# Where in the queue early loads stand, and four DMA transposes in place of eight, in an attention + two-MoE kernel

## The chip, the core and the metric

The kernel runs on one core of a Trainium2 chip. The metric is device time in microseconds (us), the median of several runs. Engines: TensorE (PE), VectorE (DVE), ScalarE (ACT), GpSimd (POOL), and SyncE (SP), whose queue issues nearly all DMAs.

## The reference

```python
mask = q_bucket[:, :, :, None] == k_bucket[:, :, None, :]
scores = np.where(mask, scale * np.matmul(q, k.transpose(0, 1, 3, 2)), -1000000000.0)
attn = np.exp(scores - np.max(scores, axis=-1, keepdims=True))
attn = attn / (np.sum(attn, axis=-1, keepdims=True) + 1e-09)
x = np.matmul(attn, v)
...
h = x @ w_in
g = np.where(h > 0.0, h, alpha * (np.exp(np.minimum(h, 0.0)) - 1.0))
x = g @ w_out
...
h = x @ w_in2
r = np.maximum(h, 0.0)
out = (s * (r * r) + b) @ w_out2
```

Attention has 2 batches, 8 heads, 768 tokens, head size 64; a bucket is the 6 sign bits of a token's projection, and a token attends only to tokens of its own bucket. Both MoE stages have 1536 tokens, 512 columns and 2048 hidden columns. The weights of both stages are float64 in memory; the other inputs are float32.

## The kernel before

**Precision.** Products run in float16 with a high and a low part (hi, lo) of each operand, three matmuls for one product. Names ending in h and l are such parts.

**Attention.** The heads of a batch come in four pairs (hp 0 to 3). `p_load` (L252) loads q, k or v of a pair; `p_split` makes hi and lo (L260, L262, L265) and issues DMA transposes to k and q (L283, L284, L292); `p_bits` (L320, L323) and `p_buck` (L333, L337) make the mask as extra columns of k and q. A unit is one head of one chunk of 128 tokens, 96 in all. Its steps: scores s (L364), row maximum p (L375) and its scaling mx (L376), exp (L377), then the transposed weights pt, then `u_av`: xacc = pt x v. The first 16 units (chunks 0 and 1) transpose on PE (L386, L389, L414, reading v itself). The others split into ph hi (ACT L396) and lo (POOL L399), go through a DMA transpose pt<-ph (L401), and use 18 matmuls with vv, the split v (L420). After the last head of a chunk `u_norm` divides (L434 to L438), makes xh (hi L450, lo on POOL L451) and puts it by DMA transposes into a token buffer xx[i] (512 tokens each, three buffers x0, x1, x2): for chunks 0 and 1 by four transposes of 2 x 128 x 128 each time (L457), for the others by one (L459). Batch 1's first pairs are loaded into the last token buffer as a guest.

**Weights of the first MoE.** `w_stream` brings w_in and then w_out in chunks of 512 KB: `w_load` (L167) loads a chunk into one of WRAW = 3 buffers wraw, DVE joins the two words of each float64 to a float32 wa (L194, L195, L197), ACT makes hi (L188), and the low part is made on DVE (L204), or, for the first ASIDE = 12 chunks of a stream, scaled and subtracted on POOL (L187, L202). A load waits until DVE is done with its buffer.

**MoE.** `moe1` runs six blocks of 256 tokens: h (L551 with wi), the activation (L559 to L574), x2p (L551 with wo), written back to the token buffers. `up2` and `down2` are the second MoE.

**What sets the order.** The program is traced in the order of the generators: the main loop steps attention and pulls one weight chunk per step until chunks 0 and 1 are done, then interleaves MoE and attention by costs. A scheduler of the compiler then puts each engine's instructions into one fixed order. Each engine runs its list in order, and so does SP's queue: a DMA that must wait holds all behind it.

```python
for _ in att:
    n += 1
    if n >= W_FROM and n % WN == 0:
        next(ws1, None)
    if done_chunks[0] == BLOCKS1[0]:
        break
...
aside_ = n_ - 3 < aside
```

Of the kernel before, what the change touches and what calls it, by code (L numbers as in the profile page):

```python
# [8 lines left out]
F16 = mybir.dt.float16  # L9
BF16 = mybir.dt.bfloat16  # L10
I32 = mybir.dt.int32
# [52 lines left out]
W_FROM = 3  # L64
LN2 = 0.6931471805599453


def model_kernel(tc, q, k, v, proj, w_in, w_out, w_in2, w_out2, s2, b2, sel, pop, eye, out):
# [24 lines left out]
    with ExitStack() as base:  # L93
# [62 lines left out]
        def w_col_chunks(dst, dram):  # L156
            w = dram.bitcast(I32)
            return [([z[:, f:f + 4, 128 * d:128 * d + 128] for z in dst],
                     w[128 * f:128 * f + 512, 256 * d:256 * d + 256].rearrange("(k p) n -> p k n", p=128))
                    for d in range(KM) for f in range(0, KF, 4)]  # L160

        def w_load(ch, wraw):
            t = wraw.tile([128, 512, 2], I32, tag="w", name="wraw")
            o = t.rearrange("p n t -> p (n t)")
            if len(ch[1].shape) == 3:
                o = o.rearrange("p (k n) -> p k n", k=ch[1].shape[1])
            nc.sync.dma_start(out=o, in_=ch[1])  # L167
            return t

        def w_stream(chunks, wraw, words, delay=0, aside=0):  # L170
            loaded, joined = [], []
            for n_, ch in enumerate(chunks + [None] * 3):
                with late_by(delay):
                    done = joined.pop(0) if joined else None
                    if done:
                        (dst, _), w = done
                        w = w.bitcast(F32)
                        if callable(dst):
                            dst = dst(w)
                            done = dst and (None, w)  # L180
# [8 lines left out]
                    if len(loaded) == 2 or (ch is None and loaded):  # L189
# [4 lines left out]
                        nc.vector.tensor_scalar(x, top, 3, 0x3FFFFFFF, op0=ALU.logical_shift_left, op1=ALU.bitwise_and)  # L194
# [47 lines left out]
        def p_load(b, hp, nm):  # L242
# [9 lines left out]
            nc.sync.dma_start(out=t, in_=a[b, 2 * hp:2 * hp + 2].rearrange("h (p c) d -> p h (c d)", c=C))  # L252
# [56 lines left out]
        def p_bits(b, hp):  # L309
# [13 lines left out]
            nc.vector.tensor_scalar(t, p, 0.0, None, op0=ALU.is_gt)  # L323
# [106 lines left out]

        def u_norm(ch):
# [7 lines left out]
            if ch < FC:  # L439
                xh = per.tile([128, FC, 2, H * D // FC], F16, tag="xh", name="xh")  # L440
                fl = xf.rearrange("p (c h) d -> p c (h d)", c=FC)
                hi, lo = xh[:, :, 0, :], xh[:, :, 1, :]
            else:
                xh = per.tile([128, 2, H * D], F16, tag="xh", name="xh")
                fl = xf.rearrange("p h d -> p (h d)")
                hi, lo = xh[:, 0, :], xh[:, 1, :]
# [12 lines left out]
            nc.sync.dma_start_transpose(out=xx[ch // 4][:, :, ch % 4 * 128:ch % 4 * 128 + 128], in_=xh.rearrange("p x d -> p (x d)"))  # L459
# [130 lines left out]
        def moe1(wi, wo, gp, next_gp, tmp, tmpg, att_step):  # L590
# [13 lines left out]
            def up(i):  # L604
# [7 lines left out]
                for f0 in range(0, KF, w_):  # L612
                    p = ring.take("m", [128, 512], F32, "h")
                    for f in range(f0, f0 + w_):
                        xs = [lambda kk, o=o: xx[i2][:, o + kk, o2:o2 + n] for o in (0, KM)]
# [9 lines left out]
            def down(i):  # L625
# [4 lines left out]
                for d0 in range(0, KM, w_):  # L630
                    p = ring.take("m", [128, w_, n], F32, "x2p")
                    for d in range(d0, d0 + w_):
                        xs = [lambda kk, z=z: z[:, kk, :] for z in g[i]]
                        ws = [lambda kk, w=w: w[:, kk, d * 128:d * 128 + 128] for w in wo]
                        for part in range(4):
                            products(p[:, d - d0, :], ws, xs, range(4 * part, 4 * part + 4), KF)
                            if part == 3 and d == d0 + w_ - 1:
                                xh, xl = (xx[i2][:, z * KM + d0:z * KM + d0 + w_, o2:o2 + n] for z in range(2))
# [52 lines left out]
        def up2(wi, g, ps_y, stream, fed, fed_all, ahead):  # L691
# [12 lines left out]
            for f in range(KF):  # L704
# [3 lines left out]
                for i in range(len(g)):  # L708
                    p = ring.take("m", [128, 512], F32, "h")
                    xs = [lambda kk, o=o: xx[i][:, o + kk, :] for o in (0, KM)]  # L710
# [118 lines left out]
        if True:  # L829
# [12 lines left out]
            n = 0  # L842
# [21 lines left out]
            ws1 = chain(ws1, w_stream(w_col_chunks(wo, w_out), *wdec))  # L864
# [135 lines left out]
```

## Time and profile before

| | |
|---|---|
| median of 3 runs | 716.72 us (714.48 to 717.6) |
| the profiled execution | 715.42 us, its span 713.6 us |
| busy share of the span | PE 92%, PEld (weight load) 70%, DVE 73%, ACT 58%, POOL 37% |
| DMA | 89.72 MB, queue of SP 57.2% of 16 engines |

The profile is one execution. Its times count from the start of the span. A row of the timeline has start, duration, engine, line, operation and tiles, and in brackets the idle time before it and what ended that. A row of stretches gives busy us of each engine in it, the granted PE clock as a share of full speed, the busy share of the DMA engines and GB/s.

### The profile page before, as it was taken

To read this page: it belongs to the slowest core of one execution; us is meant where nothing else is said; L and a number is where in the kernel's file an instruction comes from. 1 tells how busy PE (TensorE), PEld (TensorE's weight loads), DVE (VectorE), ACT (ScalarE), POOL (GpSimd) and SP (SyncE) were. 2 spreads that over 40 slices of the span, in tenths; PEclk is the share of its full clock that TensorE was granted. 3 is DMA by queue.
4 is the path that set the end of the run, shared out by engine and by line. 5 is a ranking of instruction groups with operands and counts; after the bars stand their busy time and mean duration, and the time that the engine had idled before them with its cause. 6 is when DMAs were issued, how large, how long until landed. Compare 5 with 4: busy or idle time off the path is not lost.

```text
span 713.6 us, 15219 instructions
## 1 busy us (share of the span) xinstructions
PE 656.3 (92%) x6192; PEld 501.4 (70%) x6192; DVE 521.4 (73%) x893; ACT 417.0 (58%) x687; POOL 264.8 (37%) x211
## 2 busy tenths in 40 slices
PE   2588979979888999999999999999999999999998
PEld 0367757768666777888888988874444446888887
DVE  5899999989677467745744699439999626999730
ACT  2879769867687778656755333234545525555520
POOL 0247668764444378845854421311211200000000
PEclk9899989999999999999999999999999999999999
DMA  9994689999999499766768545003443000000100
GB/s 211 325 221 139 167 197 247 217 215 211 194 217 177 82 139 169 123 119 123 123 113 117 136 155 173 1 30 119 128 143 114 0 1 1 16 31 31 45 30 30
DMA packets 206933, 89.72 MB, mean 126 GB/s; under 512 B 172048, under 2 KB 203536, under 8 KB 206864
## 3 DMA queue, kind: packets, MB, share of 16 engines
q1 hardware_dynamic: 206272, 88.63, 57.2%
q8 instruction: 48, 0.79, 0.5%
q10 hardware_dynamic: 592, 0.14, 0.1%
q14 instruction: 21, 0.17, 0.1%
HBM read 43.13 MB, written 3.15 MB: 65 GB/s over the span
## 4 chain that ended last, share of the span: by engine, by line
PE 53%; ACT 4%; DVE 4%; DMA 2%; issue 2%; POOL 1%; DVEq 0%; ACTq 0%; POOLq 0%; SPq 0%
PE h L551 23%; PE y L795 15%; PE x2p L551 10%; PE s L364 3%; PE xacc L420 2%; DVE e L566 1%; DMA pt<-ph 1%; DVE g L568 1%; ACT ph L396 1%; ACT gh L571 1%; ACT p L377 1%; POOL ph L399 1%; ACT e L559 1%; DMA wraw<-in_moe_w_in 1%; DVE p L375 1%
## 5 line engine op out<-in xcount | busy, mean ns | idle before, releaser
L399 POOL TENSOR_TENSOR ph<-p,ph 128x768 f16<-128x768 f32 x80 | 133.4, 1671 | 84.3 <-ACT ph L396 54.8
L551 PE MATMUL h<-x,wih 128*128 128x256 f16 x768 | 130.4, 274 | 0.6 <-DVE g L568 0.6
L551 PE MATMUL h<-x,wi 128*128 128x512 f16 x576 | 124.5, 379 | 0.0
L377 ACT ACTIVATE p<-p,mx 128x768 f32<-128x768 f32 x96 | 89.2, 929 | 52.3 <-DVE mx L376 42.2
L375 DVE TENSOR_SCALAR_CACHE_REDUCE p<-s 128x768 f32<-128x768 f32 x96 | 91.1, 951 | 34.2 <-PE s L364 32.4
L795 PE MATMUL y<-wqh,a 128*128 128x256 f16 x672 | 110.3, 273 | 0.0
L795 PEld LDWEIGHTS <-a 128*128 128x128 f16 x1008 | 98.6, 98 | 11.7
L551 PE MATMUL x2p<-gh,woh 128*128 128x256 f16 x384 | 104.7, 273 | 1.4 <-ACT gh L571 0.8
L551 PE MATMUL x2p<-gl,woh 128*128 128x256 f16 x384 | 104.8, 273 | 1.1 <-POOL gl L574 1.0
L551 PE MATMUL h<-x,wil 128*128 128x256 f16 x384 | 105.2, 274 | 0.0
L551 PE MATMUL x2p<-gh,wol 128*128 128x256 f16 x384 | 104.6, 273 | 0.0
L551 PEld LDWEIGHTS <-wi 128*128 128x128 f16 x576 | 56.3, 98 | 67.8
L795 PE MATMUL y<-wql,a 128*128 128x256 f16 x336 | 91.1, 273 | 0.0
L364 PE MATMUL s<-k,q 128*128 128x512 f16 (+1 forms) x384 | 81.1, 336 | 6.9 <-DVE p L375 5.6
L551 PEld LDWEIGHTS <-wih 128*128 128x128 f16 x768 | 74.8, 98 | 13.0 <-issue 1.5
L551 PEld LDWEIGHTS <-woh 128*128 128x128 f16 x768 | 74.9, 98 | 12.7 <-issue 1.0
L574 POOL TENSOR_TENSOR gl<-g,gh 128x512 f16<-128x512 f32 x48 | 57.5, 1198 | 64.0 <-ACT gh L571 63.8
L420 PE MATMUL xacc<-vv,pt 128*128 128x64 f16 x1440 | 57.3, 194 | 20.0 <-DMA pt<-ph 19.9
L396 ACT ACTIVATE ph<-p 128x768 f16<-128x768 f32 x80 | 66.6, 836 | 13.7 <-DMA pt<-ph 10.0
L420 PEld LDWEIGHTS <-pt 128*128 128x128 f16 x1440 | 52.8, 99 | 28.6 <-DMA pt<-ph 26.0
L587 DVE SCALAR_TENSOR_TENSOR g<-h,sbs,r 128x512 f32<-128x512 f32 x48 | 35.6, 744 | 23.6 <-ACT r L584 23.6
L364 PEld LDWEIGHTS <-q 128*128 128x128 f16 x384 | 34.7, 101 | 25.6 <-issue 9.7
(118 smaller groups left out, 1027.7 us busy)
## 6 DMA issues: line engine op xcount, KB each, us to landing
wraw<-in_moe_w_in SPq DMA_DIRECT2D x32, 512.0 KB, 4.0
wraw<-in_moe_w_out SPq DMA_DIRECT2D x32, 512.0 KB, 3.8
out<-y SPq DMA_DIRECT2D x10, 256.0 KB, 2.0
raw<-in_k SPq DMA_DIRECT2D x6, 384.0 KB, 4.6
raw<-in_q SPq DMA_DIRECT2D x6, 384.0 KB, 5.8
v<-in_v SPq DMA_DIRECT2D x4, 384.0 KB, 8.8
pt<-ph SPq DMA_TRANSPOSE x80, 4.1
x<-in_k SPq DMA_DIRECT2D x2, 384.0 KB, 7.3
```

The lines of the kernel that those rows point to most:

```text
L364: nc.tensor.matmul(p[:, a0:a1], w[b, hp][:, j, c, :], kf[:, a0:a1], start=(x == 0), stop=(x == 1))
L375: nc.vector.tensor_scalar(f, sps.pop(u), CLAMP, None, op0=ALU.min, op1=ALU.min, accum_out=mx)
L377: nc.scalar.activation(out=f, in_=f, func=ACTF.Exp, scale=-sm / (SQ * SQ), bias=mx, accum_out=sums[gr][:, sl:sl + 1])
L396: nc.scalar.activation(out=t[:, 0, :], in_=f, func=ACTF.Copy)
L399: nc.gpsimd.tensor_tensor(out=t[:, 1, :], in0=f, in1=t[:, 0, :], op=ALU.subtract)
L420: nc.tensor.matmul(acc, o[:, C * x + cc, :], vv[:, j, cc, y, :], start=(z == 0 and cc == 0), stop=(z == 2 and cc == C - 1))
L551: nc.tensor.matmul(p, ws[a](kk), xs[b](kk), start=(kk == 0 and z == 0), stop=(kk == n_kk - 1 and z == 2))
L559: nc.scalar.activation(out=t["e"], in_=p, func=ACTF.Exp, scale=1.0 / SG)
L566: nc.vector.tensor_scalar(t["e"], t["e"], SG, -SG, op0=ALU.mult, op1=ALU.add)
L574: nc.gpsimd.tensor_tensor(out=gl, in0=t["g"], in1=gh, op=ALU.subtract)
L587: nc.vector.scalar_tensor_tensor(out=g, in0=p, scalar=sb["s"], in1=t["r"], op0=ALU.mult, op1=ALU.mult)
L795: nc.tensor.matmul(p, a[:, xa, kk, :], wq[y][:, WQ[n], kk, :], start=first and k == 0, stop=k == 3 * K2 - 1, skip_group_check=True)
```

## The change

It makes four edits.

1. Six loads are queued behind a given load of w_in (`HOLD`, by the number of the weight load): the four v of batch 0 behind loads 3, 3, 5 and 6, and the guests k and q of batch 1 behind loads 8 and 9. One DVE instruction of the first chunk (the first of the join) is queued behind the bits of head pair 1.
2. The first two chunks of w_out are loaded into the second token buffer, which nothing uses yet, behind weight loads 10 and 11 (`HOLD_E`, `w_early`), and handed to the w_out stream as already loaded. The stream's count `n_ - 3 < aside` is then true for these two, so that their scaling and low part run on POOL.
3. In a token buffer the hi and lo parts of x stand in another order (`xb`): blocks of 128 columns come as two hi, two lo, two hi, two lo.
4. With that, chunks 0 and 1 need two transposes of 4 x 128 x 128 each time in place of four of 2 x 128 x 128.

```diff
+HOLD = {(0, 0, "v"): 3, (0, 1, "v"): 3, (0, 2, "v"): 5, (0, 3, "v"): 6, (1, 0, "k"): 8, (1, 0, "q"): 9}
+HOLD_E = [10, 11]
...
+        w_loads, pins = [], {}
+        def behind(n):
+            return tc.issue_after(w_loads[n]) if n is not None else nullcontext()
...
-            nc.sync.dma_start(out=o, in_=ch[1])
+            w_loads.append(nc.sync.dma_start(out=o, in_=ch[1]).ins)
...
+        def w_early(ch, x):
+            t = xx[1].rearrange("p a t -> p (a t)").bitcast(I32)[:, 1024 * x:1024 * x + 1024]
+            with behind(HOLD_E[x]):
+                nc.sync.dma_start(out=t.rearrange("p (k n) -> p k n", k=ch[1].shape[1]), in_=ch[1])
+            return ch, t.rearrange("p (n t) -> p n t", t=2)
...
-        def w_stream(chunks, wraw, words, delay=0, aside=0):
-            loaded, joined = [], []
+        def w_stream(chunks, wraw, words, delay=0, aside=0, loaded_=None, late_dst=False):
+            loaded, joined = list(loaded_ or ()), []
...
-                        nc.vector.tensor_scalar(x, top, 3, 0x3FFFFFFF, op0=ALU.logical_shift_left, op1=ALU.bitwise_and)
+                        with tc.issue_after(pins["bits", 0, 1]) if n_ == 2 and loaded_ is None else nullcontext():
+                            nc.vector.tensor_scalar(x, top, 3, 0x3FFFFFFF, op0=ALU.logical_shift_left, op1=ALU.bitwise_and)
...
-            nc.sync.dma_start(out=t, in_=a[b, 2 * hp:2 * hp + 2].rearrange("h (p c) d -> p h (c d)", c=C))
+            with behind(HOLD.get((b, hp, nm))):
+                nc.sync.dma_start(out=t, in_=a[b, 2 * hp:2 * hp + 2].rearrange("h (p c) d -> p h (c d)", c=C))
...
+        def xb(z, kk):
+            return 4 * (kk // 2) + 2 * z + kk % 2
...
-                    o = xx[0][:, :, 128 * c:128 * c + 128].rearrange("p (z k) t -> p z k t", z=2)
-                    for z in range(2):
-                        nc.sync.dma_start_transpose(out=o[:, z, k2 * ch:k2 * ch + k2, :], in_=xh[:, c, z, :])
+                    nc.sync.dma_start_transpose(out=xx[0][:, 2 * k2 * ch:2 * k2 * ch + 2 * k2, 128 * c:128 * c + 128],
+                                                in_=xh[:, c].rearrange("p z n -> p (z n)"))
...
+                if len(early) < len(HOLD_E) and len(w_loads) > HOLD_E[len(early)]:
+                    early.append(w_early(co1[len(early)], len(early)))
...
-            ws1 = chain(ws1, w_stream(w_col_chunks(wo, w_out), *wdec))
+            ws1 = chain(ws1, w_stream(co1[len(early):], *wdec, loaded_=early, late_dst=True))
```

**The order on SP, after the q load of head pair 3.** Before (k12, k22 and q12 are k and q of pair 2, v0 the four v, x2 the guest):

```order
L252 DMA v0_339<-in_v 128x2x384
L252 DMA v0_400<-in_v 128x2x384
L252 DMA v0_580<-in_v 128x2x384
L252 DMA v0_651<-in_v 128x2x384
L167 DMA wraw_308<-in_moe_w_in 128x4x256
L252 DMA x2_115<-in_k 128x2x384
L283 DMA_TRANSPOSE k12_347<-src_341 128x12x128
L167 DMA wraw_332<-in_moe_w_in 128x4x256
L284 DMA_TRANSPOSE k22_348<-srcl_344 128x6x128
L292 DMA_TRANSPOSE q12_356<-src_351 128x12x128
```

In the change, at the same place:

```order
L303 DMA_TRANSPOSE k12_347<-src_341 128x12x128
L304 DMA_TRANSPOSE k22_348<-srcl_344 128x6x128
L175 DMA wraw_308<-in_moe_w_in 128x4x256
L272 DMA v0_339<-in_v 128x2x384
L312 DMA_TRANSPOSE q12_356<-src_351 128x12x128
L272 DMA v0_400<-in_v 128x2x384
L303 DMA_TRANSPOSE k13_408<-src_402 128x12x128
L175 DMA wraw_332<-in_moe_w_in 128x4x256
L304 DMA_TRANSPOSE k23_409<-srcl_405 128x6x128
```

The transposes of pair 2 come first; the first v stands behind the fourth weight load (wraw_308), and the other two v and the guest come later in the list.

**The order on DVE at the first weight chunk** (wraw_226 is that chunk, bits_259 the bits of pair 1). Before:

```order
L295 COPY q21_199<-q11_197 64x768 x2
L194 TENSOR_SCALAR wx_284<-wraw_226 128x512
L195 SCALAR_TENSOR_TENSOR wx_284<-wraw_226,wx_284 128x512
L197 SCALAR_TENSOR_TENSOR wa_283<-wraw_226,wx_284 128x512
L323 TENSOR_SCALAR bits_259<-pbit_238 128x768
```

In the change:

```order
L315 COPY q21_199<-q11_197 64x768 x2
L343 TENSOR_SCALAR bits_259<-pbit_238 128x768
L213 TENSOR_SCALAR wx_284<-wraw_226 128x512
L297 COPY src_341<-src_341 128x12x64
L285 SCALAR_TENSOR_TENSOR srcl_344<-raw_272,src_341 128x6x64 x2
L395 TENSOR_SCALAR p_291,mx_292<-s_278 128x768
L285 SCALAR_TENSOR_TENSOR src_351<-raw_274,src_351 128x6x64 x2
L214 SCALAR_TENSOR_TENSOR wx_284<-wraw_226,wx_284 128x512
L396 TENSOR_SCALAR mx_292<-mx_292 128x1
L395 TENSOR_SCALAR p_334,mx_335<-s_319 128x768
L216 SCALAR_TENSOR_TENSOR wa_283<-wraw_226,wx_284 128x512
```

The bits stand ahead of the chunk, and the chunk's three passes are spread out between the splits of pair 2 and the first maxima.

**The order on POOL, at the sixth to eighth ph.** Before:

```order
L399 TENSOR_TENSOR ph_1189<-p_1184,ph_1189 128x768
L376 TENSOR_SCALAR mx_1233<-mx_1233 128x1
L376 TENSOR_SCALAR mx_1288<-mx_1288 128x1
L376 TENSOR_SCALAR mx_1347<-mx_1347 128x1
L399 TENSOR_TENSOR ph_1237<-p_1232,ph_1237 128x768
L574 TENSOR_TENSOR gl_1074<-g_1265,gh_1073 128x512
L399 TENSOR_TENSOR ph_1292<-p_1287,ph_1292 128x768
```

In the change:

```order
L419 TENSOR_TENSOR ph_1200<-p_1195,ph_1200 128x768
L396 TENSOR_SCALAR mx_1302<-mx_1302 128x1
L205 TENSOR_SCALAR wa_1132<-wa_1132 128x512
L419 TENSOR_TENSOR ph_1248<-p_1243,ph_1248 128x768
L205 TENSOR_SCALAR wa_1187<-wa_1187 128x512
L419 TENSOR_TENSOR ph_1306<-p_1301,ph_1306 128x768
L221 TENSOR_TENSOR wol_1070<-wa_1132,woh_1069 128x4x128
L396 TENSOR_SCALAR mx_1361<-mx_1361 128x1
L597 TENSOR_TENSOR gl_1072<-g_1276,gh_1071 128x512
L396 TENSOR_SCALAR mx_1394<-mx_1394 128x1
L221 TENSOR_TENSOR wol_1070<-wa_1187,woh_1069 128x4x128
```

Two scalings and two low parts of w_out (wa_1132, wa_1187) now stand among the ph.

## Rows read from the trace of the kernel before

**Rows 1.** Stretches: busy us of each engine (x instructions), PEclk, DMA share, GB/s.

```profile
20.00:84.00 64.00, 51.77 (x402) 39.58 (x397) 59.88 (x122) 51.66 (x86) 33.76 (x26) 0.95 0.80 217
50.00:80.00 30.00, 26.60 (x221) 21.53 (x220) 26.94 (x58) 25.27 (x43) 22.28 (x17) 1.00 0.52 152
84.00:96.00 12.00, 6.76 (x70) 4.82 (x69) 11.93 (x22) 7.01 (x12) 7.94 (x8) 0.88 0.86 167
96.00:160.00 64.00, 55.88 (x661) 44.57 (x660) 60.20 (x100) 52.69 (x95) 46.71 (x45) 0.95 1.07 223
110.00:120.00 10.00, 8.61 (x111) 6.83 (x109) 9.50 (x15) 8.99 (x17) 9.67 (x9) 1.00 1.23 264
160.00:240.00 80.00, 70.49 (x812) 56.16 (x811) 59.63 (x103) 61.50 (x102) 39.12 (x31) 0.99 0.98 186
301.00:713.60 412.60, 407.84 (x3498) 306.54 (x3497) 280.56 (x433) 190.85 (x307) 93.23 (x63) 1.00 0.33 78
```

**Rows 2.** Waits of PE, 84 to 240 us: total us, times, longest.

```profile
PE xacc L420 <- DMA pt<-ph: 16.6, 15, 2.7
```

**Rows 3.** Groups of DVE instructions, whole span: busy us, mean ns, idle before.

```profile
L204 DVE SCALAR_TENSOR_TENSOR wol<-wa,woh 128x512 f16<-128x512 f32 x16 | 18.7, 1170 | 2.1 <-ACT woh L188 2.1
...
L204 DVE SCALAR_TENSOR_TENSOR wi<-wa,wi 128x512 f16<-128x512 f32 x16 | 11.1, 693 | 0.0
```

**Rows 4.** Line 204, one form: min/median/max ns, first and last start.

```profile
L204 DVE SCALAR_TENSOR_TENSOR wol<-wa,woh x16: 674/1073/2034, 101.0 to 172.8; 128x512 f16<-128x512 f32 x16
```

**Rows 5.** Timeline of SP's queue from 20 us.

```profile
20.23 3.60 SPq L252 DMA_DIRECT2D v<-in_v  x4
...
26.80 6.01 SPq L283 DMA_TRANSPOSE k<-src  x1
```

**Rows 6.** Tile v of the first batch: its first reader, and its loads.

```profile
L414 PE MATMUL xacc<-v,pt x84: 220/275/323, 34.8 to 59.7; 128*128 128x64 f32 x84
...
DMA to landing us min/median/max: 8.6/8.8/9.1
```

**Rows 7.** Timeline of DVE at the first weight chunk.

```profile
20.66 0.69 DVE L194 TENSOR_SCALAR wx<-wraw 128x512 int32<-128x512 int32 x1 [2.11 <-DMA wraw<-in_moe_w_in]
...
22.12 0.69 DVE L197 SCALAR_TENSOR_TENSOR wa<-wraw,wx 128x512 int32<-128x512 int32 x1
```

**Rows 8.** DMA issues of the page: count, KB, median us to landing.

```profile
wraw<-in_moe_w_out SPq DMA_DIRECT2D x32, 512.0 KB, 3.8
...
raw<-in_k SPq DMA_DIRECT2D x6, 384.0 KB, 4.6
```

**Rows 9.** Tile xh, SP's queue: min/median/max ns, first and last start.

```profile
L457 SPq DMA_TRANSPOSE x<-xh x8: 1167/1240/2135, 69.8 to 98.0; - x8
...
L459 SPq DMA_TRANSPOSE x<-xh x4: 1232/1437/1771, 126.4 to 237.9; - x4
```

**Rows 10.** Timeline of PE at the first h matmuls.

```profile
94.64 1.14 PE L420 MATMUL xacc<-vv,pt 128*128 128x64 f16 x18 [2.68 <-DMA pt<-ph]
...
97.92 0.42 PE L551 MATMUL h<-x,wil 128*128 128x256 f16 x1
...
101.05 0.27 PE L551 MATMUL h<-x,wih 128*128 128x256 f16 x1
101.16 0.27 PE L551 MATMUL h<-x,wil 128*128 128x256 f16 x1
```

**Rows 11.** Groups of POOL instructions, 20 to 160 us: busy us, mean ns, idle before.

```profile
L187 POOL TENSOR_SCALAR wa<-wa 128x512 f32<-128x512 f32 x12 | 18.6, 1548 | 35.5 <-DVE wa L197 26.2 <-DVE mx L376 8.9
L202 POOL TENSOR_TENSOR wil<-wa,wih 128x512 f16<-128x512 f32 x12 | 13.9, 1159 | 12.1 <-ACT wih L188 11.7
```

**Rows 12.** Timeline of POOL, 105 to 111 us.

```profile
105.14 0.57 POOL L376 TENSOR_SCALAR mx<-mx 128x1 f32<-128x1 f32 x1 [1.05 <-DVE p L375]
107.81 0.19 POOL L376 TENSOR_SCALAR mx<-mx 128x1 f32<-128x1 f32 x1 [2.10 <-DVE p L375]
109.11 1.65 POOL L399 TENSOR_TENSOR ph<-p,ph 128x768 f16<-128x768 f32 x1 [1.11 <-DMA pt<-ph]
```

More of the change, by code (lines that the diff above doesn't have):

```diff
@@ L1 @@
-from contextlib import ExitStack
+from contextlib import ExitStack, nullcontext
 from itertools import chain
@@ L166, in w_load @@
                 o = o.rearrange("p (k n) -> p k n", k=ch[1].shape[1])
-            nc.sync.dma_start(out=o, in_=ch[1])
+            w_loads.append(nc.sync.dma_start(out=o, in_=ch[1]).ins)
             return t
-        def w_stream(chunks, wraw, words, delay=0, aside=0):
-            loaded, joined = [], []
+        def w_early(ch, x):
[5 more added lines that the diff above has]
+            loaded, joined = list(loaded_ or ()), []
+            if delay:
+                loaded_ = []
             for n_, ch in enumerate(chunks + [None] * 3):
@@ L177, in w_stream @@
                         w = w.bitcast(F32)
+                        if late_dst:
+                            dst = dst()
                         if callable(dst):
@@ L322, in p_bits @@
             t = ring.take("ph", [128, S], F16, "bits")
-            nc.vector.tensor_scalar(t, p, 0.0, None, op0=ALU.is_gt)
+            pins["bits", b, hp] = nc.vector.tensor_scalar(t, p, 0.0, None, op0=ALU.is_gt).ins
             bits[b, hp] = t
@@ L443, in u_norm @@
             else:
-                xh = per.tile([128, 2, H * D], F16, tag="xh", name="xh")
-                fl = xf.rearrange("p h d -> p (h d)")
-                hi, lo = xh[:, 0, :], xh[:, 1, :]
+                xh = per.tile([128, 2, 2, H * D // 2], F16, tag="xh", name="xh")
+                fl = xf.rearrange("p (y h) d -> p y (h d)", y=2)
+                hi, lo = xh[:, :, 0, :], xh[:, :, 1, :]
             if FC <= ch < C:
@@ L614, in up @@
                     for f in range(f0, f0 + w_):
-                        xs = [lambda kk, o=o: xx[i2][:, o + kk, o2:o2 + n] for o in (0, KM)]
+                        xs = [lambda kk, z=z: xx[i2][:, xb(z, kk), o2:o2 + n] for z in range(2)]
                         ws = [lambda kk, w=w: w[:, f, kk * 128:kk * 128 + 128] for w in wi]
@@ L637, in down @@
                             if part == 3 and d == d0 + w_ - 1:
-                                xh, xl = (xx[i2][:, z * KM + d0:z * KM + d0 + w_, o2:o2 + n] for z in range(2))
+                                xh, xl = (xx[i2][:, xb(z, d0):xb(z, d0) + w_, o2:o2 + n] for z in range(2))
                                 def hi(p=p, xh=xh):
@@ L709, in up2 @@
                     p = ring.take("m", [128, 512], F32, "h")
-                    xs = [lambda kk, o=o: xx[i][:, o + kk, :] for o in (0, KM)]
+                    xs = [lambda kk, z=z: xx[i][:, xb(z, kk), :] for z in range(2)]
                     ws = [lambda kk, z=z: wi(f)[:, z, kk * 128:kk * 128 + 128] for z in range(2)]
@@ L841, in model_kernel @@
             ws1 = w_stream(w_in_chunks(wi, w_in), *wdec, aside=ASIDE)
-            n = 0
+            n, early = 0, []
+            co1 = w_col_chunks(lambda: wo, w_out)
             for _ in att:
                 n += 1
+                if len(early) < len(HOLD_E) and len(w_loads) > HOLD_E[len(early)]:
+                    early.append(w_early(co1[len(early)], len(early)))
                 if n >= W_FROM and n % WN == 0:
```

4 lines of the change are left out of this document (2 added, 2 removed).

## The prediction

> **What bounds the kernel now.** I read the stretches of the program first, because one share of busy time hides stages with different limits [rows 1]. From 301 us to the end TensorE (PE) is busy 407.84 of 412.6 us: nothing the change touches can shorten that part, it can only start sooner or later. From 20 to 160 us PE is busy only 51.77 of 64, 6.76 of 12 and 55.88 of 64 us, while VectorE (DVE) is busy 59.88, 11.93 and 60.20 us of the same stretches. So DVE sets the pace up to about 160 us: it unpacks the weights, makes the splits of k, q and v, and takes the row maxima. From 160 to 240 us neither is full (PE 70.49 of 80, DVE 59.63): there the latency of a unit of attention counts, from the maximum through exp, ph, its low part on GpSimd (POOL) and the DMA transpose to the xacc matmuls.
>
> The waits of PE name the same chain: between 84 and 240 us it waits 16.6 us in 15 places for a transposed pt [rows 2]. I take this as "the unit arrives late", and ask for each edit whether it lets units arrive earlier. The order of PE's instructions in the last 3,742 matmuls is the same before and after, so a shift gained by about 240 us reaches the end in full, and one gained earlier does so unless another wait takes it.
>
> **Two low passes leave DVE.** Two chunks of w_out now stand at the head of their stream as loaded, and so its count for "aside" treats them as early: their scale and their subtraction wol go to POOL. DVE loses 2 instructions of line 204. The sixteen of them take 1170 ns each; the same shape late in the program takes 693 ns [rows 3]. I take the mean of the sixteen, as it is measured at this place: 2 x 1.17 = -2.3 us (bounds: 2 x 0.69 = -1.4, and 2 x 2.03, the longest one, = -4.1 us) [rows 4]. As DVE is the bound there, all of it is on the path.
>
> What stretches wol beside POOL is a port. The Trainium skill, SBUF — State Buffer, section Who interferes with whom, says that a DVE instruction with two SBUF inputs and a GpSimd instruction that reads SBUF exclude each other for a whole instruction; the spread from 674 to 2034 ns of one shape agrees. By that rule the four POOL passes that come in block some of the remaining wol as well; at two blocked for the difference of 0.5 us each the sum below would be 1.0 us less of a gain, 712.8 us. I leave that out of the sum and inside the range.
>
> **The order of the first loads.** Before, the four loads of v are issued back to back at 20.23 us, land only 8.6 to 9.1 us later, and the transpose of the third head pair's k behind them holds SP's queue for 6.01 us [rows 5, 6]. In the new order the k transposes of that pair stand ahead of all v loads. That brings the pair's mask earlier, but DVE has no idle time to use it: between 20 and 84 us it is idle 64 - 59.88 = 4.1 us. 2.11 us of that is the wait for the first chunk at 20.66 us, which now has one bits instruction ahead of it [rows 7]; that one needs the pbit matmuls that PE runs during just this wait, so I count nothing for it. Of the other 2.0 us I take half, -1.0 us (bounds 0 and -2.0).
>
> The first v load now waits behind the fourth load of w_in, and that waits for DVE to be done with the first chunk, whose last pass now has some eight instructions more ahead of it: an estimate of 28 us instead of 22.12 us for it [rows 7]. With 4.6 us to land, as the first loads of k, or 8.8, as v before, v is there at 33 to 38 us [rows 6, 8]; the first xacc that reads it starts at 34.8 us [rows 6]. I cost this at nothing, because PE has 12.2 us of slack in the stretch and DVE has chunks to unpack meanwhile; without that cover it is up to +3 us. The loads of x for the second batch (guests in a token buffer) and the last two v are not read for tens of microseconds: nothing.
>
> **Two chunks loaded early.** They are 2 of the 32 loads of 512 KB, 3.8 us each from issue to landing. They move from the stretch 96 to 160 us, where the DMA engines' share is 1.07, into 50 to 80 us, where it is 0.52 [rows 1, 8]. They cost nothing where they go. Where they leave, pt transposes have less beside them. Of the 16.6 us of waits I take -0.5 us (bounds 0 and -4: half of the waits shortened by 0.5 us).
>
> **Four transposes for eight.** Each of the eight takes 1.24 us of SP's queue, each of the larger four after them 1.44 us: the time hardly grows with size [rows 9]. So the second group costs about 2 x 1.4 instead of 4 x 1.24 us, and its last one, issued at 98.0 us, comes some 3 us sooner. The order on PE also changes: twelve h matmuls stand between the first and second group of xacc, where PE now waits 2.68 us at 94.64 us; afterwards they ran at the lower clock level, 0.42 us a row against 0.27 us at 101 us [rows 10]. The granted clock of 84 to 96 us is 0.88 [rows 1], a mix of the 2.4 and the 1.2 GHz level after an idle PE. Twelve matmuls at 0.11 us apart are 1.3 us that fill a wait: -1.3 us (bounds 0 and -2.7). The split of xh into two runs of 256, and token blocks read as 4(k/2)+2z+k%2, keep the elements and the 512 contiguous columns: nothing.
>
> **What POOL pays.** Two scalings at 1.55 us and two subtractions at 1.16 us are 5.4 us more on POOL [rows 11]. They stand between the sixth and the eighth ph, where POOL idles 1.05 + 2.10 + 1.11 = 4.3 us between 104 and 109 us, mostly for DVE's maxima [rows 12]; from 110 to 120 us it is busy 9.67 of 10 us [rows 1]. So 5.4 - 4.3 = 1.1 us are not covered, and the idle time shrinks where DVE comes sooner: I take +1.5 us (bounds 0 and +5.4), all on ph and so on pt.
>
> **Sum.** -2.3 - 1.0 - 0.5 - 1.3 + 1.5 = -3.6 us. The profiled execution takes 715.42 us, so 711.8 us. That execution lies 1.3 us under the median of 716.72 us (714.48 to 717.6). About 0.5%, 3.6 us, is what a measurement of this kernel can tell from no change, so the borders are 713.1 and 720.3 us.
>
> **Rivals.**
> 1. *The gain is eaten by the unit's latency.* If pt, and not DVE, sets the pace from 140 us on, work that DVE saves only makes it wait. For it: DVE idles 20 of 80 us after 160 us while PE still waits for pt. Against it: DVE is 94% busy up to there, and the same order of units on both sides means that an earlier start shifts all of them. All terms but that of POOL go to about zero: 715.4 us, inside 713.1 to 717.5.
> 2. *POOL becomes the limit (slower).* The four passes delay the seventh and later ph; PE, in order, stands at xacc, and after an idle PE the lower clock comes back. Price: 5.4 us in full and, for the stretch at half clock as at 95 to 101 us, the second half of the 5 us of work there, about 2 us, with DVE's 2.3 us taken off: +5.1, 720.5 us. It decides from the point where POOL has less than 4.3 us of idle time left between 104 and 120 us. For it: POOL is busy 46.71 of 64 us [rows 1] and would be at 52. Against it: the passes are spread among ph that wait for DVE.
> 3. *The DMA relief is larger.* If every pt lands half a microsecond sooner, as the bound above has it, and v no longer delays the early transposes, another 4 to 6 us go: 706.5 us. Against it: PE waits for pt also where the ph itself came late.
> 4. *The holds do nothing* beyond the order: then only the terms of DVE, POOL and the transposes stay, 713 us; this lies within the forecast's own range.
>
> **How the numbers follow.** Forecast 0.45 (own range 709 to 714), no gain 0.31, POOL's limit or a late v 0.16, larger relief 0.08. The range of 705 to 720.5 us takes in the ends of the last two; I leave 2 in 10 out. Faster: the forecast but for its upper end, 0.42, and the larger relief: 0.50. Slower by over 0.5%: somewhat less than rival 2, whose price lies at the border: 0.14. The same: 0.36.
>
> **What would show it.** Right: line 204's successor runs 14 times on DVE for w_out and twice on POOL; the first h starts 2 to 4 us sooner than now, right behind the xacc group of 94.64 us; the wait of 2.68 us is gone or holds h; x transposes are four, 1.4 us each; and the point from which PE is always busy comes at about 297 instead of 301 us. Wrong: the first h comes sooner but that point does not (rival 1); POOL shows no idle time from 100 to 120 us and PE's waits for pt grow over 16.6 us (rival 2); xacc waits for v near 35 us.

## The result and the profile after

The changed kernel takes 721.92 us (median of 11 runs, 719.09 to 725.22), the kernel before beside it 717.56 us (11 runs, 714.48 to 718.98): ratio 1.007, 95% interval 1.0048 to 1.0092. It is slower by 0.7%, some 5 us; 711.8 us was forecast, and 720.5 us was the end of the range. The ratios in this document are estimates over the runs of both kernels; the quotient of two medians can differ from them by up to 0.002 (here 1.006). The profiled execution took 721.27 us, with a span of 719.5 us.

The stretches of the changed kernel, as [rows 1]:

```profile
20.00:84.00 64.00, 54.09 (x399) 42.52 (x394) 56.78 (x116) 50.12 (x82) 31.95 (x24) 0.89 0.84 223
84.00:96.00 12.00, 7.10 (x58) 4.86 (x57) 10.91 (x21) 8.21 (x14) 7.71 (x9) 0.91 0.67 164
96.00:160.00 64.00, 53.56 (x612) 42.71 (x611) 56.55 (x94) 47.76 (x86) 47.45 (x45) 0.94 0.85 184
110.00:120.00 10.00, 9.89 (x105) 7.82 (x106) 5.57 (x11) 5.65 (x11) 6.75 (x9) 0.83 0.58 130
160.00:240.00 80.00, 67.88 (x805) 54.03 (x803) 62.47 (x110) 62.90 (x106) 40.27 (x35) 1.00 1.06 204
301.00:719.50 418.50, 414.18 (x3572) 312.10 (x3570) 283.90 (x442) 196.09 (x316) 98.84 (x66) 1.00 0.33 78
```

From 301 us there are 5.9 us more left than before (418.5 for 412.6), PE busy as densely: the loss was made ahead of that. From 96 to 160 us every engine did less: PE 612 matmuls for 661, DVE 94 instructions for 100, ACT 86 for 95. From 110 to 120 us DVE, ACT and POOL are busy 5.57, 5.65 and 6.75 us where they were at 9.50, 8.99 and 9.67. So DVE is no longer the bound there; PE is busy 9.89 of these 10 us, and the other three wait for what comes late from it, as the timelines below show. The waits of PE for pt, 84 to 240 us, grew from 16.6 us in 15 places [rows 2]:

```profile
PE xacc L440 <- DMA pt<-ph: 21.6, 13, 4.2
```

What the edits were to do themselves is there. Groups of DVE and POOL (busy us, mean ns), the lines of SP (min/median/max ns, first and last start), against [rows 3, 4, 9]:

```profile
L223 DVE SCALAR_TENSOR_TENSOR wol<-wa,woh 128x512 f16<-128x512 f32 x14 | 15.7, 1123 | 1.6 <-ACT woh L206 1.6
L221 POOL TENSOR_TENSOR wol<-wa,woh 128x512 f16<-128x512 f32 x2 | 2.3, 1157 | 0.1
```

```profile
L479 SPq DMA_TRANSPOSE x<-xh x4: 1247/1303/1738, 71.7 to 99.0; - x4
```

```profile
L181 SPq DMA_DIRECT2D x<-in_moe_w_out x2: 501/502/502, 67.1 to 71.1; - x2
```

Fourteen wol on DVE and two on POOL, four transposes, two early loads. The DMA engines had less to do where they were to have less (0.58 for 1.23 of 110 to 120 us), and pt transposes of 100 to 115 us land sooner. Tile pt in this window, before and then after, min/median/max from issue to landing:

```profile
DMA to landing us min/median/max: 4.9/5.6/7.0
```

```profile
DMA to landing us min/median/max: 3.8/4.3/6.3
```

So the edits arrive and the time gets worse. Where it does is read from the starts of the row maxima, one per unit of attention, here counted from 0: unit 25 starts 0.9 us sooner than before (109.9 us for 110.8), unit 26 1.3 us later (115.9, 114.6), unit 27 3.7 us (126.7, 123.0), unit 30 7.4 us (138.9, 131.5), unit 34 9.6 us (153.2, 143.6). It is lost step by step; some of it comes back, 5.0 us are left at unit 50 and 6.3 us from unit 70 on. The timeline of PE from 106 us (idle time before a group in brackets):

```profile
106.78 1.25 PE L384 MATMUL s<-k,q 128*128 128x256 f16 x7
110.11 0.61 PE L440 MATMUL xacc<-vv,pt 128*128 128x64 f16 x15 [2.08 <-DMA pt<-ph]
110.56 0.38 PE L574 MATMUL h<-x,wih 128*128 128x256 f16 x2
...
113.13 0.42 PE L574 MATMUL h<-x,wil 128*128 128x256 f16 x1
...
114.84 0.25 PE L440 MATMUL xacc<-vv,pt 128*128 128x64 f16 x3
114.93 1.46 PE L384 MATMUL s<-k,q 128*128 128x512 f16 x8
```

After a wait of 2.08 us a run of 24 h goes for the most part at the lower clock level (1.2 GHz; 0.42 us a row, as in [rows 10]; granted clock 0.83 of 110 to 120 us), and behind it stand the scores s of units 26 and 27, eight in a row. Before, they came in fours, with h between them:

```profile
113.23 0.81 PE L364 MATMUL s<-k,q 128*128 128x512 f16 x4
115.19 0.81 PE L364 MATMUL s<-k,q 128*128 128x512 f16 x4
```

The other engines of the changed kernel at this time, DVE and then ACT:

```profile
110.79 0.68 DVE L591 SCALAR_TENSOR_TENSOR g<-h,e 128x512 f32<-128x512 f32 x1
115.87 0.96 DVE L395 TENSOR_SCALAR_CACHE_REDUCE p<-s 128x768 f32<-128x768 f32 x1 [4.40 <-POOL gl L597]
...
126.67 0.95 DVE L395 TENSOR_SCALAR_CACHE_REDUCE p<-s 128x768 f32<-128x768 f32 x1
```

```profile
115.04 0.60 ACT L582 ACTIVATE e<-h 128x512 f32<-128x512 f32 x1 [2.90 <-PE h L574]
115.67 0.63 ACT L584 ACTIVATE e<-e 128x512 f32<-128x512 f32 x1
116.21 0.92 ACT L397 ACTIVATE p<-p,mx 128x768 f32<-128x768 f32 x1
```

DVE idles 4.40 us ahead of unit 26's maximum. The row names POOL's gl, which ended at 115.8 us, but that unit's scores are the first four of 114.93 us and end about then too; with the scores moved ahead (the first kernel under One group moved) the maximum comes 2.2 us behind that of unit 25 and not 6.0, so the scores held it. Between the maxima of units 26 and 27 stand fourteen other passes, where ten stood before. On ACT unit 24's exp, whose maximum had started at 108.49 us, stands behind an e that waits 2.90 us for the late h.

### The profile page after: what moved, and what is told of

The parts are those of the page before. It is cut to its first block, busy times and chain, and to the rows that moved or that the text cites. A ratio compares the mean times of both kernels' runs of the same rounds, so it can differ in the third digit from the quotient of the medians.

```text
span 719.5 us, 15222 instructions
## 1 busy us (share of the span) xinstructions
PE 659.3 (92%) x6192; PEld 504.8 (70%) x6192; DVE 518.6 (72%) x891; ACT 417.4 (58%) x687; POOL 269.5 (37%) x215
## 4 chain that ended last, share of the span: by engine, by line
PE 60%; DMA 5%; DVE 3%; ACT 2%; POOL 2%; issue 2%; SPq 1%; DVEq 0%; ACTq 0%; POOLq 0%
PE h L574 27%; PE y L818 15%; PE x2p L574 11%; DMA pt<-ph 4%; PE s L384 4%; PE xacc L440 3%; POOL ph L419 1%; DVE e L589 1%; DMA k<-src 1%; DVE g L591 1%; ACT gh L594 1%; DMA raw<-in_v 1%; DVE p L395 1%; ACT e L582 0%; ACT k L357 0%
## 5 line engine op out<-in xcount | busy, mean ns | idle before, releaser
L574 PE MATMUL h<-x,wih 128*128 128x256 f16 x768 | 133.8, 278 | 0.8 <-DMA x<-xh 0.8
```

The lines of the kernel that those rows point to most:

```text
L574: nc.tensor.matmul(p, ws[a](kk), xs[b](kk), start=(kk == 0 and z == 0), stop=(kk == n_kk - 1 and z == 2))
```

## The experiments

Five explanations stood at the start. **POOL**: the four extra passes set the units back. **HOLD**: the holds make v and the first weight late. **EARLY**: the early loads and their joins are in the way. **TRANSPOSE**: the larger transposes or the block order cost by themselves. **ORDER**: a scheduler writes the order of every engine from its own estimate of the time, any edit makes it write another, and that order costs, not the edits. The ratios are to the kernel before, on the same chip; each has an interval of about 0.0025 on either side, so a difference of two of them is uncertain by some 0.003, 2 us.

### One part undone

No two early chunks:

```diff
-HOLD_E = [10, 11]
+HOLD_E = []
```

> Edit: the changed kernel without the two early chunks of w_out, so their loads come in the stream's turn and their low passes are not on POOL; holds and four transposes stay. Theory POOL (the four extra passes of POOL between 104 and 115 us delay the units, which costs the 7 to 10 us seen behind 107 us): the loss goes, ratio to before 0.995 to 1.000, POOL has idle time again between 104 and 110 us. Theory HOLD (w_in chunks joined 3 to 6 us later and v landing 1.7 us late push everything after it): nothing changes, ratio 1.006 to 1.010. Theory ORDER (each edit only makes the scheduler write another order, and the loss is that order's stalls): any ratio from 0.995 to 1.015, with stalls at other places than in the changed kernel.

Measured: 714.88 us, 0.9973 (0.995 to 0.9996).

Early chunks, their low passes on DVE:

```diff
-                    aside_ = n_ - 3 < aside
+                    aside_ = n_ - 3 + len(loaded_ or ()) < aside
```

> Edit: the changed kernel, two early chunks still loaded early, but the scale and the subtraction of these two stay on DVE/ACT as before. Theory POOL: the loss goes as without early chunks, less the 2.3 us that DVE gets back: ratio 0.998 to 1.002. Theory EARLY (the early loads and joins themselves crowd DVE and the DMA engines before 96 us): loss stays, 1.005 to 1.012. Theory HOLD: loss stays, 1.006 to 1.012. Theory ORDER: any ratio, stalls at other places.

Measured: 712.6 us, 0.9952 (0.9926 to 0.9978).

No holds, no pinned first unpacking:

```diff
-HOLD = {(0, 0, "v"): 3, (0, 1, "v"): 3, (0, 2, "v"): 5, (0, 3, "v"): 6, (1, 0, "k"): 8, (1, 0, "q"): 9}
+HOLD = {}
...
-                        with tc.issue_after(pins["bits", 0, 1]) if n_ == 2 and loaded_ is None else nullcontext():
+                        with tc.issue_after(pins["bits", 0, 1]) if False else nullcontext():
```

> Edit: the changed kernel without the holds of six q, k and v loads and without the pinned first unpacking; early chunks and four transposes stay. Theory HOLD: the wait for v near 35 us and the late joins of w_in go, ratio 0.995 to 1.002. Theory POOL: the four passes stay on POOL, ratio 1.006 to 1.010. Theory ORDER: any ratio, stalls at other places.

Measured: 717.46 us, 1.0012 (0.999 to 1.0034).

Eight transposes and the old block order:

```diff
-        return 4 * (kk // 2) + 2 * z + kk % 2
+        return KM * z + kk
...
-                    nc.sync.dma_start_transpose(out=xx[0][:, 2 * k2 * ch:2 * k2 * ch + 2 * k2, 128 * c:128 * c + 128],
+                    for z in range(2):
+                        nc.sync.dma_start_transpose(out=o[:, z, k2 * ch:k2 * ch + k2, :], in_=xh[:, c, z, :])
```

> Edit: the changed kernel with the first outputs transposed in eight pieces as before; holds and early chunks stay. Theory POOL and theory HOLD: no gain from the undoing, ratio 1.006 to 1.012 (the 1.3 us of the four transposes are lost too). Theory TRANSPOSE (the four larger transposes or the block order make the first h late): ratio 0.995 to 1.002. Theory ORDER: any ratio, stalls at other places.

Measured: 713.28 us, 0.995 (0.9927 to 0.9972).

Undoing any one part takes the loss away, and three of the four end below the kernel before. With four costs that add up this cannot be: each undoing would gain its own share alone. The last kernel still has POOL's four passes, the holds and the early loads, so POOL, HOLD and EARLY fall as sole causes. TRANSPOSE and ORDER remain for it.

### One group moved

The order can be changed by itself. For the kernels from here on every engine's instructions are tied one behind the other with edges that set the issue order and add no wait:

```diff
+            if i is not None:
+                if last is not None:
+                    tc.add_manual_dep(i, last.name, why, reason="in order")
+                last = i
...
         model_kernel(tc, *args)
+        in_order(tc)
```

Here `why` is an edge of the class NoSync, and the order is the changed kernel's own with one or three moves. First, on PE:

```diff
-h x24 (110.56 us), xacc x3, s x8 (units 26, 27)
+s x8 (units 26, 27), h x24, xacc x3
```

> Edit: the changed kernel with every instruction at its own place in each engine's order, except on TensorE: the eight s matmuls of units 26 and 27 (at 114.93 us in the changed kernel) stand ahead of the group of 24 h matmuls at 110.56 us instead of behind it. No work is added or taken away. Theory ORDER (the loss of 8 us between 107 and 139 us is what the new order does, h ahead of the scores above all): row maxima of units 26 and 27 come some 4 us sooner, ratio to before 0.998 to 1.003. Theory POOL (the four passes on POOL set the units back whatever TensorE's order): ratio stays at 1.005 to 1.009. Theory HOLD: stays at 1.005 to 1.009.

Measured: 718.99 us, 1.0023 (1.0001 to 1.0045).

On ACT and POOL:

```diff
-ACT: e, e, exp of unit 24           POOL: wol, mx of unit 24
+ACT: exp of unit 24, e, e           POOL: mx of unit 24, wol
```

> Edit: the changed kernel in its own order, except that unit 24's exp stands ahead of the two e passes at 115.04 us on ACT, and its mx ahead of the low pass wol at 110.51 us on POOL. No work is added or taken away. Theory ORDER: exp of unit 24 at about 111.5 instead of 116.2 us, its ph 4 to 5 us sooner, the wait of 4.2 us at 127.5 us shrinks: ratio 0.998 to 1.004; if TensorE's order alone is the cause, 1.005 to 1.009. Theory POOL: the mx comes 1.2 us sooner and that is all, ratio 1.004 to 1.008. Theory HOLD: 1.005 to 1.009.

Measured: 721.24 us, 1.007 (1.0046 to 1.0094). Unit 24's exp now starts 3.6 us behind its maximum (110.1, 113.7 us) and not 7.7 (108.5, 116.2), and nothing comes of it. ACT in this kernel:

```profile
113.70 0.92 ACT L397 ACTIVATE p<-p,mx 128x768 f32<-128x768 f32 x1
...
116.72 0.60 ACT L582 ACTIVATE e<-h 128x512 f32<-128x512 f32 x1 [2.01 <-PE h L574]
117.35 0.63 ACT L584 ACTIVATE e<-e 128x512 f32<-128x512 f32 x1
119.15 0.63 ACT L206 ACTIVATE woh<-wa 128x512 f16<-128x512 f32 x1 [1.17 <-DVE wa L216]
119.69 0.83 ACT L416 ACTIVATE ph<-p 128x768 f16<-128x768 f32 x1
```

The unit's ph stands behind the same e, and behind a woh that waits for DVE, which waits for the scores behind h. The wait only moved on by one instruction.

On SP:

```diff
-wraw x2, pt of unit 24
+pt of unit 24, wraw x2
```

> Edit: the changed kernel in its own order, except on SP: the transpose of unit 24's ph stands ahead of the two w_out loads at 117.47 us instead of behind them. No work is added or taken away. Theory ORDER: this transpose at 120.6 instead of 122.2 us, a gain of at most 1.6 us, ratio 1.003 to 1.009, as ph itself is late. Theory POOL and theory HOLD: the same, 1.004 to 1.009. If the queue's order on SP alone were the cause: 0.997 to 1.001.

Measured: 721.29 us, 1.0074 (1.0049 to 1.0099). The edges themselves cost nothing that shows: these last two kernels stay at the changed kernel's ratio, and the kernel before with the larger transposes, tied to its own order in the same way, stays at 0.9999 (below).

All three:

> Edit: the three reorderings together (scores ahead of h on TensorE, unit 24's exp ahead of e on ACT and its mx ahead of wol on POOL, its transpose ahead of two loads on SP); else the changed kernel in its own order, the same work. Theory ORDER: the stretch from 107 to 139 us loses its setback, ratio 0.991 to 0.999, as the kernels with one part undone. Theory POOL: the passes still take POOL's time, ratio 1.002 to 1.008. Theory HOLD: 1.004 to 1.009.

Measured: 722.1 us, 1.0085 (1.0055 to 1.0114). ORDER as stated here, three misplaced groups, falls too: the move on PE alone gives back two thirds (0.47 of 0.70%, uncertain by 0.3), the three together nothing. The timeline of DVE in this last kernel shows one reason:

```profile
119.91 0.68 DVE L216 SCALAR_TENSOR_TENSOR wa<-wraw,wx 128x512 int32<-128x512 int32 x1
120.75 1.38 DVE L223 SCALAR_TENSOR_TENSOR wol<-wa,woh 128x512 f16<-128x512 f32 x1 [0.16 <-ACT woh L206]
124.89 0.69 DVE L213 TENSOR_SCALAR wx<-wraw 128x512 int32<-128x512 int32 x1 [2.76 <-DMA wraw<-in_moe_w_out]
...
126.68 0.95 DVE L395 TENSOR_SCALAR_CACHE_REDUCE p<-s 128x768 f32<-128x768 f32 x1
```

The transpose went ahead of two loads of w_out; one of those is now late for DVE, whose order still has that chunk ahead of unit 27's maximum. It comes at 126.68 us, in the changed kernel at 126.67 and with PE's move alone at 123.40; but these executions differ ahead of the moved groups too. Counted from unit 25's maximum it is 17.1, 16.8 and 16.4 us: by here the wait has taken back what PE's move had gained. By unit 30 the three moves are 2.3 us behind PE's alone (28.3 for 26.0 us); where the rest of that arises was not read.

### The same work in another order

The kernel with eight transposes is written in the same sequence as the changed one, so its order can be given to the changed kernel's work instruction by instruction, and the reverse; only the transposes on SP differ, two against one at each place. The two orders differ on PE at 1,710 of 6,097 matmuls, on DVE at 161 of 796 instructions, on ACT at 176 of 597, on POOL at 44 of 213, all between 99 and 308 us of the span; on SP at 34 of 223 DMAs, from 72 us on, where a load of w_in stands between the first two x transposes or behind them.

> Edit: the changed kernel's whole work (holds, early chunks, four passes on POOL, four transposes) with every engine's instructions pinned to the order that the kernel with eight transposes got (0.995 of before); each of the four transposes stands where the second of its pair stood. Theory ORDER in its wide form (not one misplaced group but the whole order after 100 us decides, row maxima of unit 27 and later behind too many joins of w_out on DVE): ratio 0.991 to 0.998. Theory TRANSPOSE (the four larger transposes cost by themselves, so undoing them gained 8 us): ratio 1.004 to 1.010. Theory POOL: 1.004 to 1.010, though the kernel with eight transposes already spoke against it.

Measured: 710.38 us, 0.9938 (0.9914 to 0.9962).

> Edit: the reverse. The kernel with eight transposes (all else changed) with every engine pinned to the order of the changed kernel; each pair of transposes stands where the one stood. Theory ORDER: the loss comes back though the transposes are undone, ratio 1.004 to 1.011. Theory TRANSPOSE: ratio 0.992 to 0.998.

Measured: 720.76 us, 1.0074 (1.0048 to 1.0101).

This decides it; the two kernels (0.9938 and 1.0074) were measured on the same chip. The changed kernel's whole work is faster than the kernel before by 0.62% in the one order and slower by 0.70% in the other; the loss stays with the order when the transposes are undone. TRANSPOSE falls, and with it every explanation by the work alone. The order is worth 1.0070 - 0.9938 = 1.3% of 716 us, 9.5 us. PE of the fast one, and DVE:

```profile
97.36 0.81 PE L384 MATMUL s<-k,q 128*128 128x512 f16 x4
98.01 0.38 PE L574 MATMUL h<-x,wih 128*128 128x256 f16 x2
98.23 0.81 PE L384 MATMUL s<-k,q 128*128 128x512 f16 x4
98.88 0.27 PE L574 MATMUL h<-x,wih 128*128 128x256 f16 x1
```

```profile
99.15 0.94 DVE L395 TENSOR_SCALAR_CACHE_REDUCE p<-s 128x768 f32<-128x768 f32 x1
...
100.62 0.94 DVE L395 TENSOR_SCALAR_CACHE_REDUCE p<-s 128x768 f32<-128x768 f32 x1
```

One of the first differences on PE is that unit 24's scores (98.23 us) stand ahead of the long run of h that begins at 98.88 us. In the changed order they stand behind its 36 matmuls, and all but the first of them behind 36 xacc too, at 106.78 us (the timeline of PE in the section on the result). So unit 24's maximum follows that of unit 23 by 1.5 us here (99.15, 100.62) and by 6.2 us there (102.3, 108.5). This is one difference of many: the kernel before, too, takes these scores behind that run. At the last unit the two profiled executions are 11.8 us apart; 3.3 us of that are there at unit 20 (92.0 and 95.3 us), ahead of the orders' first difference on the engines, and are of the kind that the last section shows between executions of one order. That leaves 8.5 us beside the 9.5 us of the ratios. PE's waits for pt, 84 to 240 us, and the stretch of 96 to 160 us:

```profile
PE xacc L440 <- DMA pt<-ph: 16.7, 11, 3.6
```

```profile
96.00:160.00 64.00, 56.57 (x695) 46.62 (x694) 57.94 (x102) 52.03 (x94) 53.51 (x51) 0.99 1.07 212
```

695 matmuls for 612, with POOL busier (53.51 for 47.45 us), not idler.

With the order held still, single terms can be priced. The low passes of two chunks, put back on POOL in the order of the kernel that has them on DVE:

> Edit: the changed kernel's whole work with PE, DVE, ACT and SP pinned to the order of the kernel that keeps the two low passes on DVE (0.9952 of before); the two low passes leave DVE, the four passes are put on POOL among the rest, whose order stays. Theory POOL: the four passes' 5.4 us come back, ratio 1.001 to 1.008. Theory ORDER: ratio 0.989 to 0.998; by the terms of the prediction DVE gains 2.3 us and POOL pays 1.5 us, so about 0.994.

Measured: 715.13 us, 0.9979 (0.9953 to 1.0006), against 0.9952: 1.9 us dearer on POOL, with intervals that overlap.

The four transposes alone, in the order of before:

> Edit: the kernel before with the four larger transposes and their block layout alone, every engine pinned to the order of before. Prediction's term: -1.3 us (0 to -2.7), ratio 0.996 to 1.000. Theory TRANSPOSE: 1.003 to 1.010. Theory ORDER says nothing of this one but that no loss can come without another order: at most 1.001.

Measured: 715.84 us, 0.9999 (0.998 to 1.0018): nothing that shows; the forecast -1.3 us lies at the edge of the interval.

### Where in the order, and on which engine

Every engine in the changed kernel's order up to a moment, and in the fast order behind it; then the reverse.

> Edit: the changed kernel's work; every engine in the changed kernel's order for the instructions that it starts before 116 us of its span (row maximum of unit 26 and what stands ahead), the rest in the order of the kernel with eight transposes. Theory EARLY ORDER (h ahead of scores and the rest of what happens up to 116 us is the loss): ratio 1.003 to 1.009. Theory LATE ORDER (the loss lies in what follows, row maximum of unit 27 behind fourteen passes of DVE): ratio 0.992 to 0.999.

Measured: 714.56 us, 0.9982 (0.996 to 1.0004).

> Edit: as the last one, but the changed kernel's order is kept up to 130 us (row maximum of unit 28). Theory LATE ORDER, with the loss between 116 and 130 us: ratio 1.003 to 1.009. If the loss arises behind 130 us: 0.992 to 0.999. Theory EARLY ORDER: 1.003 to 1.009.

Measured: 719.57 us, 1.003 (1.0007 to 1.0052).

> Edit: the reverse: the order of the kernel with eight transposes for what that kernel starts before 130 us, the changed kernel's order behind. Theories EARLY and LATE ORDER (the loss lies ahead of 130 us): ratio 0.992 to 0.999. If it arises behind 130 us: 1.003 to 1.010.

Measured: 717.35 us, 1.0019 (0.9994 to 1.0044).

Against 0.9938, the changed order costs 0.0044 (3.2 us) up to 116 us, 0.0092 (6.6 us) up to 130 us and 0.0132 (9.5 us) in all; behind 130 us alone it costs 0.0081 (5.8 us), each uncertain by some 2 us. The last kernel's ratio lies between the two ranges that I had named for it. None of the single places holds the loss: some of it arises up to 116 us, where the scores of units 24 to 27 stand behind h, and some behind 130 us; a third for each of the three stretches is the best estimate. The parts up to and behind 130 us add up to 12.4 us, 2.9 us more than the whole, which is about what they are uncertain by.

The low passes on DVE again, in the fast order:

```diff
-POOL: wa x2, wol x2 among the ph
+DVE: wol x2 among the maxima
```

> Edit: the changed kernel with the low passes of the two early chunks on DVE instead of the four on POOL, every engine in the order of the kernel with eight transposes but for these passes. Against the same order with the passes on POOL (0.9938): by the prediction's terms (DVE +2.3 us, POOL -1.5 us) 0.995; if POOL's passes are the dearer, as the other pair says (0.9952 with them on DVE, 0.9979 on POOL): 0.990 to 0.992; if neither lies on the path: 0.993 to 0.9945.

Measured: 711.18 us, 0.9948 (0.9928 to 0.9968), against 0.9938 with them on POOL: 0.7 us, the other way than in the first pair. Between the two pairs POOL's passes cost nothing that these runs can tell.

Last, one engine or two in the fast order, the others in the changed kernel's.

> Edit: the changed kernel's work and order, but SP's queue in the order of the kernel with eight transposes (loads of w_out stand otherwise among the transposes of ph). If SP's order, loads ahead of transposes that are ready, carries the loss: ratio 0.993 to 1.000. If it is the order on the engines: 1.004 to 1.010.

Measured: 726.5 us, 1.0155 (1.013 to 1.0179).

> Edit: the changed kernel's work and order on PE, POOL and SP, but DVE and ACT in the order of the kernel with eight transposes (row maxima and exp ahead of joins of w_out and of e). If DVE and ACT carry the loss: ratio 0.993 to 1.000. If PE, POOL or SP do: 1.004 to 1.010; as these still wait in their old order, a half-way result, 1.000 to 1.004, says that no engine carries it alone.

Measured: 744.11 us, 1.0401 (1.0374 to 1.0428). Both are slower than every range I had named, the latter far slower. Its waits of 96 to 160 us (total us, times, longest):

```profile
PE xacc L440 <- DMA pt<-ph: 13.8, 5, 4.6
ACT p L397 <- POOL mx L396: 10.7, 5, 7.2
DVE p L395 <- PE s L384: 7.6, 2, 4.0
POOL mx L396 <- DVE p L395: 5.6, 2, 5.2
ACT e L582 <- PE h L574: 5.6, 1, 5.6
```

DVE and ACT now ask for scores, h and mx in an order in which PE and POOL don't make them. In these two runs the orders of the engines belong together; part of the good one is worse than the whole of the bad one.

## Why the prediction was wrong

**What bounds the kernel** was read rightly only as a picture of before. DVE's 94% up to 160 us was true of that order; in the changed one it is 88% busy there (56.55 of 64 us), and no engine is full.

**Two low passes, -2.3 us, and POOL, +1.5 us.** The counts were right (14 on DVE, 2 on POOL). Their sum of -0.8 us, POOL's passes against the same work on DVE, was measured as -0.7 us in one order and +1.9 us in another, each to about 2.5 us: not refuted, not shown. The mean wol did not grow longer beside the added passes, but shorter: 1170 ns before, 1123 after, and 828 in the fast order:

```profile
L223 DVE SCALAR_TENSOR_TENSOR wol<-wa,woh 128x512 f16<-128x512 f32 x14 | 11.6, 828 | 1.5 <-ACT woh L206 1.4
```

The 1.0 us that I had worked out from the rule of the Trainium skill (SBUF — State Buffer, section Who interferes with whom) does not show in these runs; with the same passes on POOL the other order moved the mean from 1123 to 828 ns. Rival 2, POOL as the limit, came with its signs: the waits for pt rose above 16.6 us, and POOL has no idle time from 102 to 115.8 us. The first of its instructions in that stretch, the last, and the next idle time:

```profile
101.97 1.65 POOL L419 TENSOR_TENSOR ph<-p,ph 128x768 f16<-128x768 f32 x1
...
114.65 1.16 POOL L597 TENSOR_TENSOR gl<-g,gh 128x512 f16<-128x512 f32 x1
116.93 0.19 POOL L396 TENSOR_SCALAR mx<-mx 128x1 f32<-128x1 f32 x1 [1.12 <-DVE p L395]
```

It is wrong all the same: the same passes stand in the fastest order measured, with POOL busier. The signs I had named could not tell the rival from what happened.

**Order of the first loads, -1.0 us.** Not to be seen. The late v did make PE wait, 1.68 us, one of the signs named for being wrong, which I had counted as covered [rows 6]:

```profile
34.86 0.85 PE L434 MATMUL xacc<-v,pt 128*128 128x64 f32 x6 [1.68 <-DMA v<-in_v]
```

Unit 20's maximum starts at 93.4 us before; in seven profiles that have the changed kernel's order up to there it starts between 92.2 and 97.0 us. A microsecond cannot be told in that.

**Early chunks, -0.5 us.** The relief is there (median landing 4.3 for 5.6 us) though partly because the stretch does less; what it is worth by itself was not isolated, since leaving the chunks out (0.9973) changes the order too.

**Four transposes, -1.3 us.** By themselves -0.1 us (-1.4 to +1.3). The twelve h that fill a wait belong to the order, not to the transposes; the first h came 0.5 us sooner (95.14 us for 95.6), not 2 to 4, and the wait of 2.68 us ahead of the second group of xacc became one of 3.59 us ahead of the first:

```profile
94.19 1.14 PE L440 MATMUL xacc<-vv,pt 128*128 128x64 f16 x18 [3.59 <-DMA pt<-ph]
95.14 0.61 PE L574 MATMUL h<-x,wih 128*128 128x256 f16 x2
```

The sum of the queue's time was off too: 2 x 1.4 for 4 x 1.24 us is 2.2 us, where "some 3 us sooner" was written for the last transpose; it was issued 1.0 us later (99.0 us for 98.0).

**The step that failed** is the one that carried the sum to the end: "a shift gained by about 240 us reaches the end in full, and one gained earlier does so unless another wait takes it", with the note against rival 1 that "the same order of units on both sides means that an earlier start shifts all of them". The order of the units is the same, but where their scores, maxima and exp stand among h and joins is not, from 96 us on; and the 3,742 matmuls with the same order start only at about 281 us of before, not at 240. I read the new order at the places of the edits, and priced the edits; eight scores in a row behind 24 h, e ahead of unit 24's exp, fourteen passes for ten between two maxima stood in it, at none of these places. The sum had no term for the order, and that term was +9.5 us between two orders of the same work. The -3.6 us of the sum itself are near the -4.4 us (0.62% of 716) of the fast order, but this shows no more than that they can be had: that order isn't the one of before, and the changed work in the order of before was not tried. One price is wrong by its own words: with all terms but POOL's +1.5 us at zero, rival 1 gives 716.9 us, not 715.4; nothing above hangs on it.

The fast order of the changed work, 710.38 us, beats both kernels.

## What to carry to other kernels

Where a scheduler writes the order, an edit is two changes, its own work and a new order of everything behind it; here the second was worth more than all of the first. Tie the order down with edges that add no wait, and run the edit in two orders, before believing what either one says of the edit; and look in the new order, everywhere it differs, for the short instructions that start a chain (scores, maxima) standing behind long runs of filler. Don't expect to repair the order by hand: one group moved gave back some two thirds, three moved gave back nothing, and one or two engines in a good order, the others in the bad one, cost 0.8 to 3.3% more than the bad one.

## What was not expected of the hardware

Two of the kernels, with exp and with pt moved, have the same work in the same order up to 110 us, and yet their profiled executions were 4.8 us apart by unit 20's maximum (97.0 and 92.2 us). The stretch of 20 to 50 us in each, exp first and then pt first:

```profile
20.00:50.00 30.00, 23.92 (x146) 17.17 (x139) 24.20 (x47) 20.09 (x32) 8.92 (x6) 0.72 0.99 252
```

```profile
20.00:50.00 30.00, 22.40 (x152) 16.10 (x153) 26.80 (x57) 23.21 (x37) 10.27 (x7) 0.83 0.99 254
```

The granted clock differs, 0.72 and 0.83, a mix of 1.2 and 2.4 GHz; ahead of it PE had been busy 4.86 and 5.88 of the first 20 us. The two are apart much sooner than that: ACT's first pass on k, which waits for the second load of k, starts 1.9 us later in the first, with the same work ahead of it. Exp first and then pt first:

```profile
8.79 0.84 ACT L280 ACTIVATE src<-raw 128x768 f16<-128x768 f32 x1 [6.00 <-DMA raw<-in_k]
```

```profile
6.90 0.84 ACT L280 ACTIVATE src<-raw 128x768 f16<-128x768 f32 x1 [4.11 <-DMA raw<-in_k]
```

The late load is not the whole of it. In the seven profiles with this order, unit 20's maximum goes with the granted clock of 20 to 50 us: 0.89, 0.83 and 0.83 have it at 92.2, 92.2 and 92.4 us, 0.77 three times at 93.2 to 95.3, 0.72 at 97.0, and the changed kernel's own (0.77, 95.3 us) had its k as early as 6.70 us. Whether the clock is the cause here or a sign, and what sets the load apart, was not found. One profile of this kernel therefore says little of a gain of 1 or 2 us ahead of 50 us, and the verdicts above rest on ratios over 6 to 12 runs of a kernel.
